# Attention, a first feed-forward layer and a soft mixture of experts on one core: TensorE's order written out up to tile 14, with later slot transposes and sums

## The chip, the cores and the metric

The kernel runs on one core of one Trainium2 chip. The metric is the time of one execution in device microseconds (us), lower is better. Where runs are compared, the median counts.

## What is computed

Three blocks, one after the other, in float32. The reference, cut to what matters:

```python
# attention: batch 4, 8 heads, 512 local rows, 32 global rows, width 64 per head
s_g = scale * q_g @ concat(k_g, k_l).T            # global rows see everything
out_g = softmax(s_g) @ concat(v_g, v_l)
s_ll = where(|i - j| <= 32, scale * q_l @ k_l.T, -1e9)   # local rows see a band
out_l = softmax(concat(scale * q_l @ k_g.T, s_ll)) @ concat(v_g, v_l)
x = rows of concat(out_g, out_l)                  # 2176 x 512
# first layer with a product behind it
h = x @ w_in                                      # 512 -> 2048
g = maximum(0.01 * h, h)
y = g @ w_out                                     # 2048 -> 512
# soft mixture, 8 experts with 4 slots each
logits = y @ phi                                  # 2176 x 32
d = softmax of logits over the rows; slot_input = d.T @ y
slot_out[e] = maximum(slot_input[e] @ w1[e], 0) @ w2[e]   # 512 -> 1024 -> 512
out = softmax of logits over the slots @ slot_out
```

## The kernel before

The 2176 rows are worked on as 17 tiles of 128: tiles 0 to 15 are the local rows of batches 0 to 3 (four tiles each), tile 16 holds all global rows. The kernel never forms y: it multiplies `w_out` by `phi` once (`pmat`), so that the logits of a tile are `g` times `pmat`, and keeps running sums of the softmax over rows.

**Attention** runs per step, one step for two heads of a batch (four steps per batch). A step has `a_T` (transposes of keys and queries: tiles `kTp`, `qTp` in PSUM, `kT`, `qT` in SBUF), `a_S` (scores `sc`, softmax to `se`), `a_E` (transposes `etp` of the softmax, copied to `eT`) and `a_V` (product with the values into `po`, scaled into `xn`). The last steps of a batch also compute the global rows: `g_S` (scores `gl`, `gg`, softmax `gs`), `g_E` (transposes `get`, `geg`) and `g_V` (product `gpo`, scaled to `xg`, transposed as `gxt`). `step(n)` lists these pieces with weights.

**A tile** t of the first layer: `b_X` transposes its rows (`xtp`) and splits them into a high and a low part; `b_H` computes one quarter f of `h` (512 columns) in the bank `hp` with 12 matmuls, in two halves of 6, after which ScalarE writes the quarter of `g`. For the logits `g` must be transposed. For tiles 10 to 14 (`BLK`) and for the first two quarters of tiles 4 to 9 (`HALF`), `blocks` does it: a DVE transpose into `gb`, then 16 block copies per two quarters, which `MOVE` gives to GpSimd (all 16 of the first two quarters; 6 of the next two, with 5 for DVE and 5 for ScalarE). The third and fourth quarters of tiles 4 to 9 go through TensorE instead, `b_L`, into `gtp`, copied to `gT`.

**Behind the tile** come the steps that `l_items(t)` lists: `b_M` and `b_D1` (logits into `lg`, copied to `lp`), `b_D2` (column sums by a matmul on `lp`, then the exp `st` of the slot softmax on ScalarE and a part of it copied by DVE), `b_D3` (transpose of `st` into `lg`, of which DVE takes `d` and both engines take the row softmax), `b_U` (the product of `d` and `g` into the bank `up`, added to `uacc` by DVE).

PSUM has 8 banks. `tp` is a ring of two that all transposes share (`kTp`, `qTp`, `etp`, `gtp`, `xtp`, `get`, `geg`, `gxt`, and also `gg`). `hb` is a ring of two (`hp`, and `up` up to tile 6), `sc` a ring of two, `po` and `sm` (holds `lg`) one each. A bank can be written again when its last reader is done.

**Order.** ScalarE, DVE, GpSimd and the load queue run the order that a scheduler made when the program was built. For TensorE the order is that of the code inside `manual_schedule` (line 1078): there `merge` mixes the attention steps of batches 2 and 3 with `b_items`, the list of pieces of tiles 4 to 14, by their weights, and `upto` cuts the list where the next tile's transposes need attention. What is left of the list for tiles 11 to 14 (`run(*rest)`) was ordered by the scheduler, with `behind` holding some pieces back. Then tiles 15 and 16 and the experts follow.

Of the kernel before, what the change touches and what calls it, by code (L numbers as in the profile page):

```python
# [8 lines left out]
F32 = mybir.dt.float32  # L9
# [11 lines left out]
def kernel(  # L21
# [15 lines left out]
    nc = tc.nc  # L37
# [517 lines left out]
    def g_E(b):  # L555
        es, rs = gst[b]
        ets = []
        for e in range(2):
            pt = tp("get")
            for T in range(NT):  # L560
                nc.tensor.transpose(pt[:, P * T:P * T + P], es[e][:, P * T:P * T + P], ident)
            et = sa.tile([P, S], F32, tag="eT", name="get", bufs=2)
            nc.vector.tensor_copy(et, pt)
            pg = tp("geg")
            nc.tensor.transpose(pg[0:SG, 0:P], es[e][:, S:S + SG], ident)
            eg = sa.tile([SG, P], F32, tag="geg", name="geg", bufs=2)
            nc.vector.tensor_copy(eg, pg[0:SG, 0:P])
            ets.append((et, eg))
        gst[b].append(ets)

    def g_V(b):
# [3 lines left out]
        for e in range(2):  # L575
# [13 lines left out]
            in1=rs.unsqueeze(2).to_broadcast([P, 2, D]), op=ALU.mult,  # L589
        )  # L590
        pt = tp("gxt")
        nc.tensor.transpose(pt[:, 0:P], xg.rearrange("p e d -> p (e d)"), ident)
# [35 lines left out]
    def step(n):  # L628
# [10 lines left out]
        gv = (2.1, lambda: (g_V(b), load_v(n + 2) if b else None))  # L639
        return [e, (0, lambda: None), v, (1.1, lambda: g_E(b))] + ns + nt + [gv]  # L640

# [30 lines left out]
    hps = {}  # L672

    def b_H(t, f, half=None):
        xh, xl = xt[t]
# [21 lines left out]
        gs = gt[t][:, 512 * f:512 * f + 512]  # L697
        nc.scalar.activation(out=gs, in_=hp, func=AF.Prelu, alpha=0.01)  # L698
        if t in BLK or t in HALF and f < 2:
# [48 lines left out]
    def b_D1(t):  # L748
        lg = b_M(t, range(2, NQ) if t in BLK else range(NQ))
        lp = sb.tile([P, 2 * P], F32, tag="lp", name="lp", bufs=1)[:, 0:P]  # L750
        nc.vector.tensor_copy(lp, lg[:, 0:P])
        ms["lg"] = lg, lp
# [52 lines left out]
    def u_add(ds, last):  # L805

        up = bank("po", "up", 1) if last >= 7 else hb("up")
        later = "u" in ms
# [68 lines left out]
    def j_D(ts):  # L877
# [17 lines left out]
        u_add(ds, ts[-1])  # L895

    def l_items(t):
        return ([(0.0, lambda: None), (0.6, lambda: b_M(t, range(2)))] if t in BLK else [
            (0.0, lambda: None) if t in HALF else (0.9, lambda: (b_L(t, 0), b_L(t, 1))),
            (0.9, lambda: (b_L(t, 2), b_L(t, 3))),  # L900
        ]) + [
            (1.3, lambda: b_D1(t)),
            (0.3, lambda: b_D2(t)),
            (0.1, lambda: b_D3(t)),
            (1.0, lambda: b_U(t)),
        ]
# [61 lines left out]
    def b_items(t0, t1):  # L968
        its = []
        for t in range(t0, t1):  # L970
# [6 lines left out]
            if t - 1 in BLK:  # L977
                its += h[0:2] + [li[1]] + h[2:4] + [li[2]] + x + [behind(h[4])]
                its += [li[3]] + [behind(x) for x in h[5:8]] + [li[4], li[5]]
                continue  # L980
            its += [h[0], li[1], h[1], li[0], h[2], h[3], li[2]] + x + [h[4], li[3]]
            its += [h[5], h[6], li[4], h[7], li[5]]
        return its

# [92 lines left out]

    with tc.manual_schedule(engines={mybir.EngineType.PE}):
        for b in range(2, B):
            head = upto(b * NT if b == 2 else 3 * NT - 1)  # L1080
            merge(attn[b - 1], head[:-6])
            run(*head[-6:])
    actx.close()
# [85 lines left out]
    load_e(xe.tile([P, 4, CL], F32, tag="e", name="ew"), NE - 1, 4)  # L1169
    run(*rest)  # L1170
    load_next(ys, ys)

# [233 lines left out]
```

## Time and profile before

| | |
|---|---|
| runs | 497.91 us median of 3 (494.53 to 498.0) |
| profiled execution | 497.15 us, span 495.4 us |
| TensorE (PE) busy | 452.7 us, 91% |
| VectorE (DVE) busy | 277.2 us, 56% |
| ScalarE (ACT) busy | 232.9 us, 47% |
| GpSimd (POOL) busy | 160.3 us, 32% |

The span is the part of the execution that the profile covers; 1.8 us lie around it. Shares of busy time are means over stages that differ: batches 0 and 1 of attention with the conversion of the weights up to about 188 us, attention of batches 2 and 3 mixed with tiles 4 to 10 up to about 345 us, tiles 11 to 16 up to about 430 us, then the experts. In a time line each row has its start, its duration, the engine, the line of the kernel, the output and input tiles, shapes and a count. The distance between the starts of two rows shows what a piece took together with a wait behind it.

### The profile page before, as it was taken

How to read it: one execution, taken by the hardware profiler on the slowest of the kernel's cores; microseconds unless marked ns; L12 is line 12 of the kernel's file. 1: busy time of each engine (PE TensorE's matmuls, PEld its weight loads, DVE VectorE, ACT ScalarE, POOL GpSimd, SP SyncE). 2: the span in 40 equal slices, each digit the busy share in tenths (PEclk: the TensorE clock that was granted, in tenths of full speed). 3: DMA queues.
4: the chain of work that ended last, by engine and by line, in shares of the span. 5: the costliest groups of instructions: out<-in, count | busy, mean ns of one | idle time of the engine just before them, and what ended most of it. 6: DMA issues, size and time to landing. Idle time of an engine off the chain costs nothing.

```text
span 495.4 us, 13462 instructions
## 1 busy us (share of the span) xinstructions
PE 452.7 (91%) x5341; PEld 319.9 (65%) x5341; DVE 277.2 (56%) x880; ACT 232.9 (47%) x678; POOL 160.3 (32%) x281
## 2 busy tenths in 40 slices
PE   7968799998989999999879999999999999999982
PEld 5635668676766656776648776778687777743341
DVE  4575879489547677477544656525655532242222
ACT  4666789487755445453144446124434343321021
POOL 2044787333310203541505161506666630000000
PEclk9985699999999999999989999999999999999998
DMA  9999688499655755344331220259320059989997
GB/s 176 215 197 235 218 254 334 161 304 296 211 144 118 147 115 102 72 103 114 76 75 32 58 54 8 86 213 404 150 85 1 2 173 329 384 336 400 348 301 256
DMA packets 111990, 90.23 MB, mean 182 GB/s; under 512 B 75256, under 2 KB 94392, under 8 KB 111928
## 3 DMA queue, kind: packets, MB, share of 16 engines
q1 hardware_dynamic: 110024, 88.33, 61.4%
q10 hardware_dynamic: 1904, 1.05, 0.8%
q8 instruction: 42, 0.69, 0.6%
q14 instruction: 20, 0.16, 0.1%
HBM read 76.68 MB, written 8.65 MB: 172 GB/s over the span
## 4 chain that ended last, share of the span: by engine, by line
PE 65%; DVE 8%; ACT 4%; DMA 3%; SPq 1%; issue 1%; POOL 1%; DVEq 0%; ACTq 0%; POOLq 0%
PE hp L691 31%; PE gtp L728 4%; PE sc L434 3%; PE up L812 3%; PE po L493 2%; PE lg L742 2%; PE ehp L1270 2%; DMA ew<-in_moe_w_dram 2%; DVE se L446 2%; PE etp L473 2%; ACT se L454 2%; PE sop L1304 1%; SPq L1127 1%; PE wotp L345 1%; PE gpo L579 1%
## 5 line engine op out<-in xcount | busy, mean ns | idle before, releaser
L691 PE MATMUL hp<-wi,xxh 128*128 128x512 f32 x512 | 168.5, 411 | 1.5 <-ACT xxh L665 1.4
L691 PEld LDWEIGHTS hp<-wi,xxh 128*128 128x128 f32 x512 | 93.3, 193 | 28.3 <-issue 6.6
L719 POOL COPY g<-gb 32x256 f32<-32x256 f32 x206 | 82.4, 400 | 83.5 <-DVE gb L710 53.5
L691 PE MATMUL hp<-wi,xxl 128*128 128x512 f32 x256 | 101.9, 399 | 0.0
L698 ACT ACTIVATE g<-hp 128x512 f32<-128x512 f32 x60 | 35.5, 594 | 57.6 <-PE hp L691 54.3
L454 ACT ACTIVATE se<-se,nmx 128x128 f32<-128x128 f32 x128 | 49.6, 390 | 15.6 <-DVE nmx L452 15.5
L691 PEld LDWEIGHTS hp<-wi,xxl 128*128 128x128 f32 x256 | 48.9, 191 | 11.7 <-issue 0.8
L200 POOL COPY vw<-vw 32x1664 f32<-32x1664 f32 x10 | 15.7, 1574 | 81.7 <-DMA vw<-in_v_g_dram 39.5
L710 DVE STREAM_TRANSPOSE gb<-g 128x512 f32<-128x512 f32 x32 | 22.6, 708 | 26.0 <-ACT g L698 25.8
L446 DVE CUSTOM_DVE_ANT_0 se<-sc,mask 128x128 f32<-128x128 f32 x128 | 28.8, 285 | 14.1 <-PE sc L434 14.0
L261 POOL TENSOR_TENSOR wn<-wn,rraw 128x512 int32<-128x512 int32 x16 | 23.0, 1448 | 37.9 <-DVE wn L257 31.3
L434 PE MATMUL sc<-kw,qT 64*32 64x128 f32 x1024 | 27.5, 283 | 1.2 <-DVE kw L406 0.5
L261 POOL TENSOR_TENSOR wo<-wo,rraw 128x512 int32<-128x512 int32 x12 | 16.0, 1330 | 32.0 <-DVE wo L257 7.2
L477 DVE COPY eT<-etp 128x512 f32<-128x512 f32 x28 | 18.6, 687 | 11.4 <-PE etp L473 11.4
L434 PEld LDWEIGHTS sc<-kw,qT 64*32 64x32 f32 x1024 | 19.7, 109 | 8.0 <-issue 4.2
L493 PE MATMUL po<-vw,eT 128*32 128x64 f32 x1024 | 21.9, 229 | 2.8 <-issue 2.0
L730 ACT COPY gT<-gtp 128x512 f32<-128x512 f32 x26 | 14.9, 585 | 20.1 <-PE gtp L728 17.6
L454 ACT ACTIVATION_READ_ACCUMULATOR se<-se,nmx 128x1 f32 x128 | 24.1, 189 | 0.0
L493 PEld LDWEIGHTS po<-vw,eT 128*32 128x32 f32 x1024 | 17.5, 115 | 9.3 <-issue 6.7
L473 PE MATMUL etp<-identr,se 128*128 128x128 f32 x128 | 22.4, 300 | 0.2
L405 DVE COPY kw<-kT 128x672 f32<-128x672 f32 x32 | 19.8, 653 | 3.0 <-ACT kT L394 2.6
L251 ACT ACTIVATE rraw<-rraw 128x512 int32<-128x512 uint32 x28 | 18.7, 676 | 4.4 <-DMA rraw<-in_moe_w_out_dram 3.0
(228 smaller groups left out, 765.5 us busy)
## 6 DMA issues: line engine op xcount, KB each, us to landing
ew<-in_moe_w_dram SPq DMA_DIRECT2D x23, 1024.0 KB, 9.4
rraw<-in_moe_w_in_dram SPq DMA_DIRECT2D x16, 512.0 KB, 6.5
ew<-in_moe_w_dram SPq DMA_DIRECT2D x15, 512.0 KB, 8.8
vw<-in_v_l_dram SPq DMA_DIRECT2D x60, 112.0 KB, 3.3
rraw<-in_moe_w_out_dram SPq DMA_DIRECT2D x12, 512.0 KB, 6.0
wo_f<-wo SPq DMA_DIRECT2D x16, 256.0 KB, 3.9
vn<-in_v_l_dram SPq DMA_DIRECT2D x4, 1024.0 KB, 6.2
wo<-wo_f SPq DMA_DIRECT2D x4, 1024.0 KB, 8.0
```

What stands on the lines that cost most here:

```text
L261: nc.gpsimd.tensor_tensor(out=di, in0=di, in1=m, op=ALU.add)
L405: nc.vector.tensor_copy(kw[:, :, 0:96], src)
L434: last_a[0] = nc.tensor.matmul(bks[e][32 * u:32 * u + 32, P * T:P * T + P], qt[64 * e:64 * e + 64, 32 * U:32 * U + 32], kw[win(U) // (NW / ...
L446: nc.vector.tensor_tensor_reduce(out=s[:, T, :], in0=bk[:, P * T:P * T + P], in1=mask[:, 0 if T == 0 else 2 if T == NT - 1 else 1, :], sca ...
L454: exp_last[0] = nc.scalar.activation(out=s[:, T, :], in_=s[:, T, :], func=AF.Exp, bias=nmx[:, e, T:T + 1], accum_out=sm[:, T, e:e + 1],).ins
L473: last_a[0] = nc.tensor.transpose(pt[:, P * T:P * T + P], es[e][:, T, :], ident).ins
L493: last_a[0] = nc.tensor.matmul(pov[32 * u:32 * u + 32, T, e, :], ets[e][:, 32 * U:32 * U + 32], vw[:, win(U), e, :], start=True, stop=True ...
L691: nc.tensor.matmul(hp, a[:, k, :], w[c][:, k, :], start=(n == 0 and half != 1), stop=(n == len(prods) - 1 and half != 0),)
L698: nc.scalar.activation(out=gs, in_=hp, func=AF.Prelu, alpha=0.01)
L710: nc.vector.transpose(out=gb[:, f % 2], in_=gs)
L719: copy(dst[32 * c:32 * c + 32, :, a], src[32 * a:32 * a + 32, :, c])
L728: nc.tensor.transpose(pt[:, P * c:P * c + P], g[:, o:o + P], ident)
```

## The change

The change has five parts, all in the work on tiles 4 to 14.

1. `b_items` writes another order. The transpose of `st` (`b_D3`) and the product `up` (`b_U`) of tile t, which closed the list of tile t + 1, move into the list of tile t + 2, behind its first and its second half quarter; for tiles 10 to 14 only `b_U` moves. The two halves of the logits (first quarters by `blocks`, second by `gT` or `blocks`) are two pieces also for tiles 4 to 9. `behind` is gone from the list.
2. `manual_schedule` stays open until the list of tiles up to 14 has run, so tiles 11 to 14 are in written order as well.
3. For batches 2 and 3, `step` splits the global pieces: `g_E` makes only the two `get`s, `g_G` both `geg`s later, and `g_X` the transpose `gxt` after another piece.
4. `ahead` gives the scheduler a higher priority for the evictions of `hp`, the copy `lp`, and the steps behind `b_D2` and `b_D3` of tiles 4 to 14.
5. `up` of tiles 4 to 6 takes the bank `po` in place of the ring `hb`.

The diff, cut to its core:

```diff
@@ g_E, g_G, g_V, g_X
-            pg = tp("geg")
-            nc.tensor.transpose(pg[0:SG, 0:P], es[e][:, S:S + SG], ident)
...
+            ets.append([et])
+            if b < 2:
+                g_G(b, e, ets)
...
+        gst["x"] = xg
+        if b < 2:
+            g_X(b)
@@ step
-        return [e, (0, lambda: None), v, (1.1, lambda: g_E(b))] + ns + nt + [gv]
+        if b < 2:
+            return [e, (0, lambda: None), v, (1.1, lambda: g_E(b))] + ns + nt + [gv]
+        gg = (0.3, lambda: [g_G(b, e, gst[b][2]) for e in range(2)])
+        return [e, v, (0.8, lambda: g_E(b))] + ns + [gg] + nt + [gv, (0.1, lambda: g_X(b))]
@@ priorities
+    def ahead(t):
+        return tc.high_priority(offset=400) if NT <= t < NTT - 2 else ExitStack()
...
+    def first(f, t):
+        with ahead(t):
+            f(t)
@@ b_D1, u_add, l_items
-        lg = b_M(t, range(2, NQ) if t in BLK else range(NQ))
+        lg = b_M(t, range(2, NQ) if t in BLK or t in HALF else range(NQ))
...
-        up = bank("po", "up", 1) if last >= 7 else hb("up")
+        up = bank("po", "up", 1) if last >= NT else hb("up")
...
-            (0.0, lambda: None) if t in HALF else (0.9, lambda: (b_L(t, 0), b_L(t, 1))),
+            (0.6, lambda: b_M(t, range(2))) if t in HALF else (0.9, lambda: (b_L(t, 0), b_L(t, 1))),
...
-            (0.3, lambda: b_D2(t)),
-            (0.1, lambda: b_D3(t)),
+            (0.3, lambda: first(b_D2, t)),
+            (0.1, lambda: first(b_D3, t)),
@@ b_items
-                its += h[0:2] + [li[1]] + h[2:4] + [li[2]] + x + [behind(h[4])]
-                its += [li[3]] + [behind(x) for x in h[5:8]] + [li[4], li[5]]
+                its += [h[0]] + d3 + [h[1]] + u + [li[1]] + h[2:4] + [li[2]] + x + [h[4]]
+                its += [li[3]] + h[5:8] + [li[4]]
+                d3, u = [], [li[5]]
                 continue
-            its += [h[0], li[1], h[1], li[0], h[2], h[3], li[2]] + x + [h[4], li[3]]
-            its += [h[5], h[6], li[4], h[7], li[5]]
-        return its
+            its += [h[0]] + d3 + [h[1]] + u + [li[1], h[2], h[3], li[0]] + x + [h[4], li[2]]
+            its += [h[5], li[3], h[6], h[7]]
+            d3, u = [li[4]], [li[5]]
+        return its + d3 + u
@@ the mixed stage
-    with tc.manual_schedule(engines={mybir.EngineType.PE}):
+    mctx = ExitStack()
+    mctx.enter_context(tc.manual_schedule(engines={mybir.EngineType.PE}))
...
     run(*rest)
+    mctx.close()
```

What this does to the order of the instructions, at three places. The first is TensorE at tile 5 and the last attention step of batch 2: from the column sums (`lg<-lp`) over the transposes of keys and queries to `up`. Runs of first-layer matmuls (`hp`) are cut to "...". Before:

```order
L757 MATMUL lg<-lp,s_77 128x128
...
L390 MATMUL kTp<-identr,kn 128x128 x4
L390 MATMUL qTp<-identr,qn 128x128 x4
L802 MATMUL lg<-identr,st 128x128
...
L592 MATMUL gxt<-identr,xg 128x128
L812 MATMUL up<-g,d 32x512 x4
```

After:

```order
L572 MATMUL geg<-identr,gs 32x128 x2
L777 MATMUL lg<-lp,s_77 128x128
L390 MATMUL kTp<-identr,kn 128x128 x4
L390 MATMUL qTp<-identr,qn 128x128 x4
...
L604 MATMUL gxt<-identr,xg 128x128
L822 MATMUL lg<-identr,st 128x128
...
L832 MATMUL up<-g,d 32x512 x4
```

The transpose of `st` has moved from right behind `qTp` to behind `gxt`: between the column sums and it stand now the key and query transposes, one half quarter, the forty matmuls of `gpo`, two more half quarters and `gxt`. In front of the column sums the scores `sc` stood directly; now two half quarters, a piece of `lg` and both `geg`s stand between.

The second place is DVE at the step before it in batch 2, around the addition to `uacc` of tile 4. Before:

```order
L819 SCALAR_TENSOR_TENSOR uacc<-uacc,al,up 128x512
L549 TENSOR_SCALAR gsms<-gsms 128x2
L550 RECIPROCAL grs<-gsms 128x2
L405 COPY kw<-kT 128x7x96 x2
L406 COPY kw<-kgT 128x7x32 x2
L501 TENSOR_TENSOR xn<-po,rs 128x4x128
L730 COPY gT<-gtp 128x512
L477 COPY eT<-etp 128x512 x2
```

After:

```order
L839 SCALAR_TENSOR_TENSOR uacc<-uacc,al,up 128x512
L477 COPY eT<-etp 128x512
L729 STREAM_TRANSPOSE gb<-g 128x512
L477 COPY eT<-etp 128x512
L749 COPY gT<-gtp 128x512
```

The addition to `uacc` stood ahead of the key windows `kw`, an attention output and `gT`; now it stands directly ahead of the copies that empty `etp`, with a transpose into `gb` between them. On TensorE `up`, `etp` and `gtp` follow each other there.

The third place is TensorE at the global scores of batch 3, `gl` and `gg`. Before:

```order
L473 MATMUL etp<-identr,se 128x128 x8
L728 MATMUL gtp<-identr,g 128x128 x8
L519 MATMUL gl<-kT,qgT 32x512 x4
L525 MATMUL gg<-kgT,qgT 32x32 x4
L519 MATMUL gl<-kT,qgT 32x512 x4
L525 MATMUL gg<-kgT,qgT 32x32 x4
L691 MATMUL hp<-wi,xxh 128x512 x2
```

After:

```order
L473 MATMUL etp<-identr,se 128x128 x8
L822 MATMUL lg<-identr,st 128x128
...
L519 MATMUL gl<-kT,qgT 32x512 x4
L525 MATMUL gg<-kgT,qgT 32x32 x4
L519 MATMUL gl<-kT,qgT 32x512 x4
L525 MATMUL gg<-kgT,qgT 32x32 x4
L832 MATMUL up<-g,d 32x512 x4
L747 MATMUL gtp<-identr,g 128x128 x8
```

`gtp` has moved from ahead of the global scores to behind them, with only `up` of tile 7 between; the three half quarters that followed `gg` have moved elsewhere. `gg` and `gtp` share the ring `tp`.

## Rows read from the trace of the kernel before

**Rows 1.** Table by stage: stretch, length, busy us (instructions), PEclk, DMA share, GB/s.

```profile
345.00:400.00 55.00, 55.00 (x376) 40.44 (x374) 32.87 (x88) 22.12 (x60) 34.16 (x85) 1.00 0.19 72
400.00:490.00 90.00, 81.88 (x807) 46.92 (x799) 26.86 (x71) 22.13 (x52) 1.19 (x4) 1.00 0.95 332
```

**Rows 2.** Waits of TensorE from 186 to 380 us: total us, times, longest.

```profile
PE lg L802 <- DVE st L767: 3.8, 2, 3.1
PE get L561 <- DVE get L563: 1.4, 2, 0.7
PE gxt L592 <- DVE xg L587: 0.9, 2, 0.5
PE up L812 <- ACT gs L536: 0.8, 1, 0.8
PE xtp L659 <- ACT kT L394: 0.6, 2, 0.3
```

**Rows 3.** Time line of TensorE, 248 to 256 us: start, us, row, count, wait.

```profile
248.84 0.60 PE L390 MATMUL qTp<-identr,qn 128*128 128x128 f32 x4
252.50 0.48 PE L802 MATMUL lg<-identr,st 128*128 128x128 f32 x1 [3.06 <-DVE st L767]
252.63 1.20 PE L691 MATMUL hp<-wi,xxh 128*128 128x512 f32 x2
...
255.47 0.67 PE L579 MATMUL gpo<-vn,get 128*32 128x64 f32 x32
```

**Rows 4.** Time line of ScalarE at the same place.

```profile
248.51 0.40 ACT L454 ACTIVATE se<-se,nmx 128x128 f32<-128x128 f32 x1 [0.67 <-DVE nmx L452]
...
251.60 0.34 ACT L766 ACTIVATE st<-lg,nm 128x128 f32<-128x128 f32 x1
```

**Rows 5.** Table by stage behind that wait (PEclk is the third figure from the end).

```profile
253.00:254.00 1.00, 1.00 (x3) 0.77 (x3) 0.99 (x3) 0.09 (x1) 0.00 (x0) 0.50 0.00 0
```

**Rows 6.** Time line of TensorE at the global rows of batch 2.

```profile
239.87 0.27 PE L565 MATMUL geg<-identr,gs 128*32 128x128 f32 x1
240.81 0.66 PE L561 MATMUL get<-identr,gs 128*128 128x128 f32 x4 [0.68 <-DVE get L563]
```

**Rows 7.** Time line of TensorE: a pair of transposes, then undisturbed work.

```profile
301.59 1.03 PE L473 MATMUL etp<-identr,se 128*128 128x128 f32 x8
...
304.22 1.23 PE L519 MATMUL gl<-kT,qgT 64*32 64x512 f32 x16
...
326.17 0.73 PE L691 MATMUL hp<-wi,xxh 128*128 128x512 f32 x2
...
326.97 0.62 PE L691 MATMUL hp<-wi,xxh 128*128 128x512 f32 x2
...
327.66 1.04 PE L728 MATMUL gtp<-identr,g 128*128 128x128 f32 x8
328.45 0.71 PE L691 MATMUL hp<-wi,xxh 128*128 128x512 f32 x2
```

**Rows 8.** TensorE behind `gg` of batch 3, then ScalarE emptying its banks.

```profile
305.44 0.73 PE L691 MATMUL hp<-wi,xxh 128*128 128x512 f32 x2
...
307.12 0.28 ACT L542 ACTIVATE gs<-gg,gnmx 128x32 f32<-128x32 f32 x1
...
308.05 0.29 ACT L542 ACTIVATE gs<-gg,gnmx 128x32 f32<-128x32 f32 x1
```

**Rows 9.** Time line of DVE: what it does with banks that TensorE filled.

```profile
228.02 0.74 DVE L819 SCALAR_TENSOR_TENSOR uacc<-uacc,al,up 128x512 f32<-128x512 f32 x1
...
231.21 0.69 DVE L501 TENSOR_TENSOR xn<-po,rs 128x512 f32<-128x512 f32 x1 [0.87 <-PE po L493]
...
302.23 1.29 DVE L477 COPY eT<-etp 128x512 f32<-128x512 f32 x2 [1.24 <-PE etp L473]
```

**Rows 10.** GpSimd's copies of a first half of g, then TensorE's `up`.

```profile
363.36 6.94 POOL L719 COPY g<-gb 32x256 f32<-32x256 f32 x16 [3.36 <-PE lg L742]
...
371.99 1.06 PE L812 MATMUL up<-g,d 128*32 128x512 f32 x8
```

More of the change, by code (lines that the diff above doesn't have):

```diff
@@ L563, in g_E, with g_G @@
             nc.vector.tensor_copy(et, pt)
-            pg = tp("geg")
-            nc.tensor.transpose(pg[0:SG, 0:P], es[e][:, S:S + SG], ident)
-            eg = sa.tile([SG, P], F32, tag="geg", name="geg", bufs=2)
-            nc.vector.tensor_copy(eg, pg[0:SG, 0:P])
-            ets.append((et, eg))
-        gst[b].append(ets)
+            ets.append([et])
+            if b < 2:
+                g_G(b, e, ets)
+        gst[b].append(ets)
+    def g_G(b, e, ets):
+        es = gst[b][0]
+        pg = tp("geg")
+        nc.tensor.transpose(pg[0:SG, 0:P], es[e][:, S:S + SG], ident)
+        eg = sa.tile([SG, P], F32, tag="geg", name="geg", bufs=2)
+        nc.vector.tensor_copy(eg, pg[0:SG, 0:P])
+        ets[e].append(eg)
     def g_V(b):
@@ L590, in g_V, with g_X @@
         )
+        gst["x"] = xg
+        if b < 2:
+            g_X(b)
+    def g_X(b):
+        xg = gst.pop("x")
         pt = tp("gxt")
@@ L697, in b_H @@
         gs = gt[t][:, 512 * f:512 * f + 512]
-        nc.scalar.activation(out=gs, in_=hp, func=AF.Prelu, alpha=0.01)
+        with ahead(t):
+            nc.scalar.activation(out=gs, in_=hp, func=AF.Prelu, alpha=0.01)
         if t in BLK or t in HALF and f < 2:
@@ L748, in b_D1 @@
     def b_D1(t):
-        lg = b_M(t, range(2, NQ) if t in BLK else range(NQ))
+        lg = b_M(t, range(2, NQ) if t in BLK or t in HALF else range(NQ))
         lp = sb.tile([P, 2 * P], F32, tag="lp", name="lp", bufs=1)[:, 0:P]
-        nc.vector.tensor_copy(lp, lg[:, 0:P])
+        with ahead(t):
+            nc.vector.tensor_copy(lp, lg[:, 0:P])
         ms["lg"] = lg, lp
@@ L895, in j_D @@
         u_add(ds, ts[-1])
+    def first(f, t):
+        with ahead(t):
+            f(t)
     def l_items(t):
         return ([(0.0, lambda: None), (0.6, lambda: b_M(t, range(2)))] if t in BLK else [
-            (0.0, lambda: None) if t in HALF else (0.9, lambda: (b_L(t, 0), b_L(t, 1))),
+            (0.6, lambda: b_M(t, range(2))) if t in HALF else (0.9, lambda: (b_L(t, 0), b_L(t, 1))),
             (0.9, lambda: (b_L(t, 2), b_L(t, 3))),
@@ L968, in b_items @@
     def b_items(t0, t1):
-        its = []
+        its, d3, u = [], [], []
         for t in range(t0, t1):
@@ L1076, in upto @@
         return head
-    with tc.manual_schedule(engines={mybir.EngineType.PE}):
[L1079 to L1082, printed above, removed]
+    mctx = ExitStack()
+    mctx.enter_context(tc.manual_schedule(engines={mybir.EngineType.PE}))
+    for b in range(2, B):
+        head = upto(b * NT if b == 2 else 3 * NT - 1)
+        merge(attn[b - 1], head[:-6])
+        run(*head[-6:])
     actx.close()
```

## The prediction

> **What bounds the kernel now.** I looked at the page's busy times first: TensorE is busy 91% of the span and no other engine passes 56%, so the question is where TensorE stands still, and in which stage. The table by stage then splits the run [rows 1]. From 345 to 400 us TensorE is busy for all 55.00 us at the full clock, while the DMA engines are busy 0.19 of the time. From 400 us on, the DMA engines are busy 0.95 of the time, moving expert weights, and this stage begins only when TensorE's last tiles free the buffers of the first layer's weights. So what TensorE saves before 400 us should move the whole last stage earlier. The savings must come from 188 to 345 us, where attention of batches 2 and 3 is mixed with first-layer tiles 4 to 10.
>
> The list of waits of TensorE [rows 2] names the stops there: two on DVE's copy of `st` (3.1 and about 0.7 us), two on the copy of `get`, two before `gxt`, one `up` behind the softmax of the global rows. Busy time hides more of them, because matmuls are pipelined, so from here on I compare starts: the time from one row's start to the next, against the same work where nothing disturbs it.
>
> The largest stop, read closely. Between the start of the four `qTp` transposes and the transpose of `st` 3.66 us pass [rows 3], and four such transposes take about 0.42. The cause stands on ScalarE [rows 4]: the exp of `st` runs at 251.60, behind the eight softmax exps that began at 248.51. And the stop costs twice: behind it the granted clock reads 0.50, its lower level of 1.2 GHz [rows 5], so that the next half quarter of the first layer (six matmuls) takes 2.84 us, from 252.63 to 255.47 [rows 3], where 1.49 is usual, 326.17 to 327.66 [rows 7].
>
> **What the change removes.** All terms are of TensorE's own time line.
> - Transpose of `st` of tile 5: from the second to the last step of a tile's chain into the next tile. Now `kTp`, `qTp`, three half quarters, `gpo` (about 2 us) and `gxt` lie between the column sums and it, some 7 us, and ScalarE's order has its exp behind the same exps, but those begin earlier relative to it, because `sc` now stands ahead of two half quarters, `lg` and `geg`. 3.66 - 0.42 = 3.25 us, and the half clock behind it, 2.84 - 1.49 = 1.35 us.
> - `get` and `geg`: before, `geg` took a bank of the two-bank ring `tp` between the two `get`s, so 0.94 us pass from one `geg` to the next `get` [rows 6], of which the transpose itself needs about 0.11. Three such places (two at batch 2, one at batch 3): 3 x 0.83 = 2.5 us. Now both `get`s run together, and `geg` runs after a half quarter. The wait of `xtp` on the second of them is one of the three; with `lg` of 0.46 between, I keep at most 0.05.
> - `gxt`: two half quarters stand ahead of it now, 0.9 us for the two [rows 2].
> - Waits of `up` and the second wait on `st`: 0.8 + 0.7 = 1.5 us [rows 2]. `up` of tiles 4 to 6 leaves the ring `hb`, so it no longer waits for a bank that ScalarE empties behind the global softmax.
> - The pair of `etp` and `gtp`, sixteen transposes one after the other: 2.63 us from 301.59 to 304.22, against 0.79 for eight, 327.66 to 328.45 [rows 7]: 1.05 lost. The same pair stands at tile 4 in the order of before, and I count 0.9 for it. Both pairs are parted.
> Sum removed: 3.25 + 1.35 + 2.5 + 0.9 + 1.5 + 1.95 = 11.45 us.
>
> **What it adds.**
> - Tile 4: `gtp` right behind `kTp` and `qTp`. Of `xtp` in the same position two waits of 0.3 are listed [rows 2]; with what busy time hides of the second bank I take 0.5 us.
> - Tile 5 (batch 2): `up`, `etp`, `gtp` in a row, and DVE's order is `uacc`, `eT`, a transpose into `gb`, `eT`. Let `etp` start at E. `uacc` (0.74) holds DVE until about E + 0.85, the first copy (0.65, of two in 1.29) until E + 1.5, `gb` (as large a tile, so 0.7) until E + 2.2, the second copy until E + 2.85 [rows 9]. The last four transposes of `gtp` so end near E + 3.3 instead of E + 1.6: 1.7 us. If DVE comes to `uacc` early and `gb` waits elsewhere, it is 0.4; if TensorE drops to half clock behind it, 1.7 + 1.35 = 3.05.
> - Tile 8 (batch 3): `gl`, `gg`, `up`, `gtp`. `gg` lies in the ring that `gtp` wants. Before, `gg` ended at 305.44 and its two banks were read out by 307.4 and 308.4 [rows 8], 2.0 and 3.0 us later; that was free, because three half quarters and more followed. Now only `up` (1.0) follows, and ScalarE's new order puts one eviction of `g` (0.5 to 0.6) between the two, so 3.5 for the second bank. `gtp` ends at about 3.9 instead of 1.8 us behind `gg`: 2.1 us. Bounds: 0.9 if only the first bank counts, 3.45 with the half clock.
> - Smaller: `kTp` behind `geg` (0.25), `qTp` behind `etp` at tile 6 (0.2), `up` of tile 4 behind `d` (0.15): 0.6 us, bounds 0 and 2.
> - TensorE changes four times more often between a first-layer run and something else, and a restart costs about 0.1: of a half quarter the first three matmuls take 0.80 us and the next three 0.69 [rows 7]. With the halved `lg` I take 0.5 us.
> Sum added: 0.5 + 1.7 + 2.1 + 0.6 + 0.5 = 5.4 us.
>
> **What costs nothing, and its cover.** From tile 10 on, the first half of `lg` runs 2.9 us earlier. It needs the sixteen GpSimd copies of that half: 363.36 + 6.94 = 370.3, and it would stand behind `up`, which starts at 371.99 and takes 1.0 [rows 10]. That leaves 2.7 us of cover. `up` after the second half quarter also delays the first eviction of the next tile (the buffer `g` has two turns) by 1 us, covered by the three half quarters until that bank returns. Loads are triggered by the same transposes as before, and nothing in [rows 2] waits for one.
>
> Sum against the profiled run's own time: 497.15 - 11.45 + 5.4 = 491.1 us; that run lies 0.8 below the median of 497.91, within their spread, so I leave it at 491.1.
>
> **A bank shared.** `up` of tiles 4 to 6 now shares the one bank `po` with the attention outputs. DVE's product into `xn` empties `po` and takes 0.69 us [rows 9]; with some 0.15 until it starts, an `up` right behind `po` would stop for about 0.85, three of them for 2.5. In the new order at least a half quarter (1.49) and the transpose of `st` stand between, so I charge only the 0.15 above. The Trainium skill, "Perfetto Trace Analysis", section "Matmuls" under tensor performance, says that independent matmul groups should rotate through different PSUM banks, so that one is emptied while the next group runs; by that rule leaving the ring of two banks is a step back, and the sum would be 493.6 instead of 491.1. No row here shows an `up` behind `po` on one bank in these tiles.
>
> **Rivals.**
> 1. *The waits only change place.* With two banks for all transposes, each eviction that DVE or ScalarE reaches late is a stop. If both new stops reach the length at which the clock falls (3.05 + 3.45), the small ones cost 2, and one more stop of 1.5 shows up, 5.4 becomes 11.0: 496.7 us. For it: DVE's and ScalarE's orders were changed by priority, and `sm`, which needs all eight exps, now stands ahead of `eT` at tile 6. Against: the slack that I count at the other places is 0.5 us or more at all but two.
> 2. *`up` stops for `po`*, three times 0.85: 493.6 us. For it: DVE often stands in other work when `po` ends. Against: the half quarter between.
> 3. *The new stops hardly show* (0.4, 0.9, and 0 of the small ones): 5.4 becomes 2.3, 488.0 us.
> 4. *The gain does not arrive at the end.* If the DMA stage after 400 us ran by the landing of its loads alone, the end would stay at 497. Against: those loads cannot start before TensorE frees their buffers.
> 5. *Slower: DVE's order starves the ring.* Eight attention steps each pass two evictions through DVE behind softmax sums. If that stop is like the one of [rows 3] with its clock (3.25 + 1.35 = 4.6), then two such places already cost more than the gain, 500.3, and from three on the kernel is slower by over 1%: 491.1 + 3 x 4.6 = 504.9 us. The slack that I count at those places is 0 to 3 us, so a single one is possible, three are not likely.
>
> **How the numbers follow.** Forecast 0.53 (488.5 to 493.5 alone), rival 1 0.17, rival 2 0.05, rival 3 0.12, rival 4 0.06, rival 5 0.07. The predicted time is 491.1. The range 487.0 to 496.8 leaves out rival 5, most of 4 and the low end of 3. Within 1% of 497.9 (492.9 to 502.9) is about what a measurement of this kernel cannot tell from no change. Faster: most of the forecast (0.46) and rival 3, 0.58; same: the rest of the forecast, rivals 1, 2 and 4, 0.35; slower: rival 5, 0.07.
>
> **What would show it.** In the profile after: no stop over 1 us before a transpose of `st`, and a granted clock of 1.00 in all of batch 2's attention; starts of `get` and `get` 0.45 apart; a stop of about 1 us and another inside `gtp` behind `gg` at batch 3, and a slow `etp`/`gtp` pair at batch 2; TensorE reaching tile 11 some 6 us earlier, and the same length from there to the end. Wrong would be: the clock at 0.50 in a new place, TensorE waiting on GpSimd copies before `lg` in tiles 10 to 14, or a last stage longer than before.

## The result, and the profile after

The changed kernel takes 490.13 us (median of 4 runs, 489.67 to 491.9) against 497.64 us (4 runs), a ratio of 0.987 with the 95% interval 0.982 to 0.992. A second series of the same code gave 492.4 us (6 runs, 489.57 to 493.89) against 497.76 us and the same ratio, 0.987 (0.982 to 0.992). The gain of 1.3% is thus clear of no change; that it is over 1% is likely and not certain. The profiled execution takes 490.33 us with a span of 488.6 us; TensorE is busy 451.3 us of it, 92%. The forecast of 491.1 us stands 1.0 us off the first series and 1.3 us off the second.

Where the 6.8 us of span went is read between two rows that both kernels have: the last `up` ahead of the mixed stage (its operand is `gx`), and `up` of tile 13. The time line of TensorE after:

```profile
185.95 1.06 PE L832 MATMUL up<-gx,d 128*32 128x512 f32 x8
...
392.75 1.06 PE L832 MATMUL up<-g,d 128*32 128x512 f32 x8
```

That is 206.80 us. Before:

```profile
186.91 1.06 PE L812 MATMUL up<-gx,d 128*32 128x512 f32 x8
...
399.51 1.06 PE L812 MATMUL up<-g,d 128*32 128x512 f32 x8
```

That is 212.60 us. So the changed stretch is 5.8 us shorter, and another 1.0 us lies ahead of it, where the order is the same; over the fourteen traces of this case the first of the two rows starts anywhere from 185.5 to 187.4, so that 1.0 is spread and no effect. From the second row to the end of the span it is 95.85 us after and 95.89 before.

The list of TensorE's waits from 186 to 400 us (total us, times, longest), to be laid beside [rows 2]:

```profile
PE gtp L747 <- ACT gs L542: 1.9, 2, 1.2
PE gtp L747 <- DVE eT L477: 1.0, 2, 0.5
PE xtp L674 <- ACT kT L394: 0.5, 2, 0.3
PE xtp L674 <- DVE eT L477: 0.4, 1, 0.4
...
```

The waits on `st`, `get` and `xg` are gone. New are two pairs, both at `gtp`: behind `gg`, on the exp `gs`, and behind `etp`, on `eT`. (Before, too, `gtp` waited for `eT`, 0.7 us in two, but at other pairs, those of tiles 4 and 8, which the change parts.) The table by stage (stretch, length, busy us of TensorE, its weight loads, DVE, ScalarE and GpSimd, then granted clock, DMA share and GB/s) has them in its second and third row:

```profile
186.00:230.00 44.00, 43.40 (x582) 32.97 (x579) 27.33 (x110) 21.93 (x79) 17.63 (x35) 1.00 0.41 82
230.00:260.00 30.00, 28.98 (x435) 21.19 (x433) 17.13 (x54) 10.49 (x34) 9.46 (x18) 1.00 0.46 108
260.00:300.00 40.00, 37.84 (x534) 27.97 (x519) 26.39 (x112) 21.82 (x83) 16.05 (x34) 1.00 0.19 37
...
345.00:400.00 55.00, 54.75 (x374) 40.59 (x373) 31.30 (x82) 23.59 (x59) 32.95 (x82) 1.00 0.15 51
```

The granted clock is 1.00 in all of them; the half clock of [rows 5] does not occur. Where the 3.06 us stop of [rows 3] stood, the transpose of `st` passes without a wait, 0.02 us from its start to the next:

```profile
252.22 0.27 PE L604 MATMUL gxt<-identr,xg 128*128 128x128 f32 x1
252.33 0.27 PE L822 MATMUL lg<-identr,st 128*128 128x128 f32 x1
252.35 0.71 PE L709 MATMUL hp<-wi,xxh 128*128 128x512 f32 x2
```

The first new stop, at tile 5, in the time line of TensorE:

```profile
229.53 1.06 PE L832 MATMUL up<-g,d 128*32 128x512 f32 x8
230.52 1.09 PE L473 MATMUL etp<-identr,se 128*128 128x128 f32 x8
232.06 0.66 PE L747 MATMUL gtp<-identr,g 128*128 128x128 f32 x4 [0.45 <-DVE eT L477]
233.26 0.66 PE L747 MATMUL gtp<-identr,g 128*128 128x128 f32 x4 [0.54 <-DVE eT L477]
233.67 0.70 PE L709 MATMUL hp<-wi,xxh 128*128 128x512 f32 x2
```

And in that of DVE, which empties the two banks of the ring `tp`:

```profile
230.66 0.75 DVE L839 SCALAR_TENSOR_TENSOR uacc<-uacc,al,up 128x512 f32<-128x512 f32 x1
231.32 0.68 DVE L477 COPY eT<-etp 128x512 f32<-128x512 f32 x1
231.92 0.70 DVE L729 STREAM_TRANSPOSE gb<-g 128x512 f32<-128x512 f32 x1
232.55 0.65 DVE L477 COPY eT<-etp 128x512 f32<-128x512 f32 x1
```

DVE's four rows run without a gap, and the last `gtp` starts when the fourth is through: sixteen transposes take 3.15 us, from 230.52 to 233.67. The second, at the global scores of batch 3, on TensorE:

```profile
296.01 0.29 PE L525 MATMUL gg<-kgT,qgT 64*32 64x32 f32 x16
296.24 1.06 PE L832 MATMUL up<-g,d 128*32 128x512 f32 x8
298.45 0.66 PE L747 MATMUL gtp<-identr,g 128*128 128x128 f32 x4 [1.15 <-ACT gs L542]
299.88 0.66 PE L747 MATMUL gtp<-identr,g 128*128 128x128 f32 x4 [0.77 <-ACT gs L542]
```

And on ScalarE, whose two exps `gs` empty the banks of `gg`:

```profile
298.03 0.28 ACT L542 ACTIVATE gs<-gg,gnmx 128x32 f32<-128x32 f32 x1
...
298.29 0.59 ACT L717 ACTIVATE g<-hp 128x512 f32<-128x512 f32 x1
...
299.43 0.30 ACT L542 ACTIVATE gs<-gg,gnmx 128x32 f32<-128x32 f32 x1
```

`gtp` is through at 300.29, 4.05 us after `up` began right behind `gg`, where `up` and eight transposes alone would take 1.8.

### The profile page after: what moved, and what is told of

Its sections match the earlier page's. It is cut to its first block, busy times and chain, and to the rows that moved or that the text cites. A ratio compares the mean times of both kernels' runs of the same rounds, so it can differ in the third digit from the quotient of the medians.

```text
span 488.6 us, 13462 instructions
## 1 busy us (share of the span) xinstructions
PE 451.3 (92%) x5341; PEld 316.7 (65%) x5341; DVE 275.7 (56%) x880; ACT 234.2 (48%) x678; POOL 160.0 (33%) x281
## 3 DMA queue, kind: packets, MB, share of 16 engines
q10 hardware_dynamic: 1904, 1.05, 0.8%
## 4 chain that ended last, share of the span: by engine, by line
PE 74%; ACT 7%; DMA 6%; DVE 5%; SPq 4%; issue 2%; POOL 1%; DVEq 0%; ACTq 0%; POOLq 0%
PE hp L709 37%; DMA rraw<-in_moe_w_in_dram 4%; PE gtp L747 3%; PE sc L434 3%; PE ehp L1298 3%; PE up L832 3%; PE po L493 2%; PE lg L761 2%; PE etp L473 2%; PE xtp L674 1%; PE wotp L345 1%; PE sop L1332 1%; SPq L162 1%; PE gpo L585 1%; ACT se L454 1%
## 5 line engine op out<-in xcount | busy, mean ns | idle before, releaser
L709 PEld LDWEIGHTS hp<-wi,xxh 128*128 128x128 f32 x512 | 92.1, 191 | 24.2 <-issue 5.3
L747 PE MATMUL gtp<-identr,g 128*128 128x128 f32 x112 | 16.9, 281 | 4.7 <-ACT gs L542 1.9
```

The lines of the kernel that those rows point to most:

```text
L709: nc.tensor.matmul(hp, a[:, k, :], w[c][:, k, :], start=(n == 0 and half != 1), stop=(n == len(prods) - 1 and half != 0),)
L747: nc.tensor.transpose(pt[:, P * c:P * c + P], g[:, o:o + P], ident)
```

## The experiments

The theory: the gain is the sum of stops removed, less the two new stops at `gtp`. Against it stood that the gain comes from one part alone, that the shared bank `po` eats some of it, and that the parts thought to be free are not. In the table "stretch" is the distance between the two rows named above. Each group of four lines is set against the kernel before on its own chip: medians 497.04 us for the first four lines, 497.93 for the next four, 497.76 for the last four.

| kernel | us | ratio to before (95%) | stretch, us |
|---|---|---|---|
| glob_whole: changed kernel, global steps whole | 496.1 | 0.999 (0.995 to 1.002) | 211.90 |
| before_split: kernel before, global steps split | 490.15 | 0.983 (0.979 to 0.987) | 207.30 |
| slots_early: changed kernel, `st` and `up` not later | 501.78 | 1.008 (1.004 to 1.011) | 217.08 |
| gt_sel: changed kernel, two `gtp` one half quarter later | 488.3 | 0.979 (0.974 to 0.984) | 204.50 |
| no_prio: changed kernel, no priorities | 493.4 | 0.991 (0.989 to 0.994) | 209.58 |
| up_hb: changed kernel, `up` in ring `hb` | 492.2 | 0.988 (0.983 to 0.993) | 208.36 |
| slots_early_hb: slots_early, `up` in ring `hb` | 501.56 | 1.006 (1.003 to 1.009) | 217.08 |
| gt_sel_hb: gt_sel, `up` in ring `hb` | 488.28 | 0.980 (0.977 to 0.984) | 204.22 |
| after_again: the changed kernel | 492.4 | 0.987 (0.982 to 0.992) | 207.18 |
| sched_tail: changed kernel, tiles 11 to 14 scheduled | 522.96 | 1.049 (1.043 to 1.056) | - |
| lg_whole: changed kernel, `lg` of tiles 4 to 9 in one piece | 497.62 | 1.001 (0.998 to 1.004) | 212.26 |
| gt_sel2: gt_sel, `gtp` of tile 8 two half quarters later | 486.38 | 0.977 (0.972 to 0.983) | 203.34 |

(A dash: the scheduler gives `up` of tile 13 another place there, with 97.9 us to the end of the span instead of 95.1 to 96.2, so the distance would compare different work.)

### The split of the global steps, taken out and done alone

Taken out of the changed kernel (glob_whole), and put alone into the kernel before (before_split, which gets the new `g_E`, `g_G`, `g_X` and `step` and nothing else). The edit of glob_whole:

```diff
-            if b < 2:
-                g_G(b, e, ets)
+            g_G(b, e, ets)
...
-        if b < 2:
-            g_X(b)
+        g_X(b)
...
-        if b < 2:
+        if True:
             return [e, (0, lambda: None), v, (1.1, lambda: g_E(b))] + ns + nt + [gv]
```

> The changed kernel with the global steps of batches 2 and 3 whole again, as before the change (get, geg, get, geg in a row, gxt right behind gpo). Theory (each geg between the two get costs 0.83 us of a bank, each gxt 0.45): 3 to 4 stops of 0.8 and two of 0.45 come back, 3.3 us or more: 493.4 us; the transpose of st of tile 5 still has no stop and the clock stays at 1.00. Rival (the gain is all in the later slots): 490.1 us.

> The kernel before with one part of the change alone: the global steps of batches 2 and 3 split. Theory (stops add up by place): the three stops of 0.83 us around get and geg go, the stops of gxt too (0.9 us in all), and because the column sums of tile 5 now come behind kTp and qTp and gpo stands between them and the transpose of st, most of the 3.25 us stop with its half clock (1.35 us) goes as well: 497.6 - 2.5 - 0.9 - 3.5 = 490.7, up to 493 if the stop only moves. Rival (without the later slots the stop of st stays whole, with the half clock): 494.3 us.

glob_whole gives back 5.1 us of stretch (211.90 against 206.80), more than its theory expected (3.3 us or more, 493.4 us against the 496.1 measured), and its list of waits names the places:

```profile
...
PE get L561 <- DVE get L563: 1.4, 2, 0.7
...
PE gxt L602 <- ACT qT L394: 0.9, 1, 0.9
PE etp L473 <- DVE eT L477: 0.8, 1, 0.8
...
PE gxt L602 <- DVE xg L592: 0.4, 1, 0.4
```

No wait on `st` is listed, so the rest of the change removes that stop without the split. But before_split removes most of it too, without any later slot: what was 3.06 us [rows 3] is 0.74 there, and the clock stays at 1.00.

```profile
PE lg L817 <- DVE st L782: 1.5, 2, 0.8
PE gtp L743 <- DVE eT L477: 0.7, 2, 0.3
...
```

The time line of ScalarE there shows why (first of the eight softmax exps, then the exp of `st`):

```profile
242.47 0.40 ACT L454 ACTIVATE se<-se,nmx 128x128 f32<-128x128 f32 x1 [0.77 <-DVE nmx L452]
...
245.57 0.35 ACT L781 ACTIVATE st<-lg,nm 128x128 f32<-128x128 f32 x1
```

The scores `sc` now stand ahead of `xtp` and no longer behind two `geg`s, so the softmax exps begin 0.18 us behind the start of the column sums (242.29). Before, they began 3.19 us behind it (245.32 to 248.51, [rows 4]), and the exp of `st` waited for them. Split alone: a ratio of 0.983. All parts: 0.987. All parts but the split: 0.999. So the split carries the gain, and the other four parts together add nothing that these runs can tell from zero. That zero is a balance: they remove the stop on `st` as well, and bring in the two stops at `gtp`. With these taken away (gt_sel2 below), the stretch is 4.0 us shorter than with the split alone (203.34 against 207.30).

### The later places of `st` and `up`, and the bank of `up`

slots_early keeps everything but the later places. up_hb is the changed kernel with `up` of tiles 4 to 6 back in its old ring, and slots_early_hb has both edits:

```diff
...
-            its += [h[0]] + d3 + [h[1]] + u + [li[1], h[2], h[3], li[0]] + x + [h[4], li[2]]
-            its += [h[5], li[3], h[6], h[7]]
-            d3, u = [li[4]], [li[5]]
+            its += [h[0], h[1], li[1], h[2], h[3], li[0]] + x + [h[4], li[2]]
+            its += [h[5], li[3], h[6], li[4], h[7], li[5]]
...
-        up = bank("po", "up", 1) if last >= NT else hb("up")
+        up = bank("po", "up", 1) if last >= 7 else hb("up")
```

> The changed kernel with the transpose of st and up back at the end of the next tile's list; split global steps, priorities and written tail stay. Theory (the later place takes the exp of st off TensorE's line): a stop of about 2.2 us before the transpose of st right behind the global scores of batch 2, and one near 1 us at tile 6; at tile 8 up no longer stands in front of gtp but a half quarter does, so 1 to 1.5 us of that stop go, and the stop of up, etp, gtp at tile 5 shrinks to 1; 491.5 to 492.5 us, and half clock only if a stop reaches 3 us. Rival A (the later slots carry most of the gain): 494.5 us or more. Rival B (the priority has the exp early enough anyway): 490 us or less.

> The kernel with the last transposes of a tile's chain and its up inside the next tile as before (501.8 us), now also with up of tiles 4 to 6 in the ring hb. Theory (the shared bank po is one part of its loss, the two stops of 1.40 and 0.81 us at po and up; the stops on st, 3.9 us, and the 0.7 us per tile at tiles 11 to 13 stay): 499.6 us. Rival (the bank also drives the stops on st, because DVE waits in it): 496 us or less. Rival 2 (the bank is beside the point): 501.8 us.

> The changed kernel with the product up of tiles 4 to 6 back in the ring hb of the first layer's banks, so that it no longer shares the bank po with the attention outputs; orders of TensorE, ScalarE and DVE the same. Theory (in the changed kernel up stands at least one half quarter behind po, so the shared bank costs nothing): 490 us, within 1 us of the changed kernel. Rival (the shared bank costs up to 0.85 us at each of three tiles, hidden in busy time): 487.5 to 489 us. Third: ring hb is then short of a bank and hp stops: 491 to 492 us.

slots_early is slower than the kernel before, and 9 us slower than its theory had it; only rival A (494.5 us or more) leaves room for it. Its waits:

```profile
PE lg L822 <- DVE st L787: 3.9, 3, 2.0
PE po L493 <- DVE uacc L839: 1.4, 1, 1.4
...
PE up L832 <- DVE xn L501: 0.8, 1, 0.8
...
```

The new order puts the column sums one half quarter later; with `b_D3` left in its old place only one half quarter of matmuls lies between the column sums and the transpose, and the stops on `st` come back. In tiles 11 to 13 `up` now follows the transpose of `st` directly and waits 0.28 us for `d`, and each of these tiles takes 14.85 us from `up` to `up` instead of 14.14. The later places are thus what the rest of the new order needs, not a gain on top of it. The second and third line are the shared bank: where `up` and `po` follow each other directly, one waits for DVE to empty the bank of the other. In slots_early_hb both are gone, and from `up` to the next row at that place it is 0.88 us instead of 2.46. Yet the kernel is no faster (501.56 us, the number of the rival by which the bank is beside the point), and the stretch is 217.08 us in both traces. Two things took the gain back in the trace. One is a new stop on `st` at tile 6, ahead of the place where `up` no longer waits for `po`:

```profile
273.21 0.33 PE L822 MATMUL lg<-identr,st 128*128 128x128 f32 x1 [0.61 <-DVE st L787]
```

The other is the clock: behind the same 2.00 us stop on `st` just ahead of this place it stayed at 1.00 in slots_early and fell to 0.50, the level of 1.2 GHz, in slots_early_hb (table by stage):

```profile
227.00:228.00 1.00, 1.00 (x3) 0.79 (x3) 0.53 (x3) 0.37 (x2) 0.00 (x0) 0.50 0.00 0
```

so that the next six matmuls took 2.71 us instead of 1.46. The expectation of slots_early tied the half clock to a stop of 3 us; 2.00 us was enough here. How far the clock explains the medians, and not only these two traces, is not shown.

In the changed kernel itself the bank costs nothing. From `up` of one tile to that of the next, for tiles 4 to 7, up_hb takes 24.38, 20.60 and 21.70 us and the changed kernel 24.39, 20.61 and 21.71. Its trace is 1.6 us longer for another reason, again the clock: orders, and the stops of 1.15 and 0.77 us at `gtp` of tile 8, are the same, and behind them the table reads, first up_hb (whose stop ends at 302.01), then the changed kernel (300.29), in which no such stretch from 150 to 400 us is below 1.00:

```profile
302.00:303.00 1.00, 1.00 (x4) 0.82 (x3) 0.00 (x0) 0.59 (x1) 0.00 (x0) 0.50 0.06 16
```

```profile
302.00:303.00 1.00, 1.00 (x65) 0.91 (x59) 0.00 (x0) 0.00 (x0) 0.00 (x0) 1.00 0.00 0
```

The six matmuls behind the stop took 2.75 us in up_hb and 1.56 in the changed kernel. The median of 492.2 us is near the number that the third expectation gave to a ring short of a bank, but the list of waits has none of `hp`.

### Priorities, the piece of `lg`, the written order of tiles 11 to 14

Three parts that the forecast took to be worth nothing, each undone alone. First the priorities, then the piece of `lg` (its weight in the list goes too), then the written order:

```diff
-        return tc.high_priority(offset=400) if NT <= t < NTT - 2 else ExitStack()
+        return tc.high_priority(offset=400) if False else ExitStack()
```

> The changed kernel without its priorities (the Prelu of the first layer, the copy lp and the two routing steps are no longer put ahead for tiles 4 to 13); TensorE's order stays the same row for row, and only some ten rows of ScalarE and thirty of DVE stand elsewhere. Theory (the priorities hardly matter, since TensorE stopped nowhere on lp, d or the Prelu in the changed kernel): 490 us, within 1 us of the changed kernel, list of waits the same to within 0.5 us. Rival (they are what keeps the Prelu and lp ahead of the softmax work): stops of hp on the Prelu or of lg on lp appear, 493 us or more.

```diff
-        lg = b_M(t, range(2, NQ) if t in BLK or t in HALF else range(NQ))
+        lg = b_M(t, range(2, NQ) if t in BLK else range(NQ))
...
-            (0.6, lambda: b_M(t, range(2))) if t in HALF else (0.9, lambda: (b_L(t, 0), b_L(t, 1))),
+            (0.0, lambda: None) if t in HALF else (0.9, lambda: (b_L(t, 0), b_L(t, 1))),
```

> The changed kernel with the routing product lg of tiles 4 to 9 in one piece again, behind the second slot transposes, instead of a first half ahead of them. Theory (the split of lg fills no gap of its own; it only moves 0.55 us of matmuls): 490 us, within 1 us of the changed kernel. Rival (the first half of lg is what stands between etp, get, or gg and the next transposes, and hides DVE's copies there): xtp waits for eT at two or three places by 0.5 us more, 491 to 492 us.

```diff
+    mctx.close()
     actx.close()
...
     run(*rest)
-    mctx.close()
```

> The changed kernel with the written order of TensorE ended after the mixed stage, so that tiles 11 to 14 of the first layer are ordered by the scheduler again, as before the change; the stage up to 330 us is the same. Theory (that part of the change is worth nothing, since TensorE was busy without a break there before too): 490 us, within 1 us of the changed kernel. Rival (the written order saves stops there): 492 us or more, with waits of up or lg in the list from 345 to 400 us.

All three theories (that the part is worth nothing) were wrong. **Without the priorities** TensorE's order is the same, but at tile 7 the exp of `st` stands behind the eight softmax exps again, and DVE copies `eT` ahead of `st`. The list of waits shows a stop that the changed kernel does not have, and two others grow:

```profile
...
PE lg L822 <- DVE st L787: 1.3, 1, 1.3
PE xtp L674 <- ACT kT L394: 1.2, 2, 0.9
...
PE lg L761 <- ACT ce L814: 0.7, 1, 0.7
...
```

The rival has the number (493 us or more) but not the cause: its stops of `hp` and on `lp` did not come. The stretch is 2.8 us longer than in the first trace of the changed kernel and 2.4 longer than in its second; the intervals of the ratios (0.989 to 0.994, and 0.982 to 0.992) overlap, so the size rests on the traces.

**With `lg` in one piece** all of the gain is lost, more than the rival's 491 to 492 us. TensorE stops for 3.26 us at `etp` of the second step of batch 3:

```profile
282.47 1.14 PE L473 MATMUL etp<-identr,se 128*128 128x128 f32 x8 [3.26 <-ACT gT L749]
```

ScalarE shows what is late (the last of the eight exps, then the two copies that empty the ring):

```profile
281.47 0.39 ACT L454 ACTIVATE se<-se,nmx 128x128 f32<-128x128 f32 x1
...
281.85 1.04 ACT L749 COPY gT<-gtp 128x512 f32<-128x512 f32 x2
```

In the changed kernel these two copies ran at 276.28, ahead of the exps. The piece itself need not be the cause: without its weight the merge put `etp` one half quarter closer to `gtp`, and the scheduler then put the exps first on ScalarE; no run keeps the weight without the piece. So this run shows the price of that order (3.3 us, six matmuls at 2.61 us behind it, and 1.1 us at another `etp`), and not that a split `lg` is worth it anywhere else.

**With tiles 11 to 14 left to the scheduler** the kernel is 5% slower; the rival (492 us or more, waits of `lg` and `up`) has the kind of loss but not its size. TensorE runs all 24 matmuls of a half tile together and the chain of small steps behind the logits together too, with nothing in between:

```profile
360.11 0.48 PE L822 MATMUL lg<-identr,st 128*128 128x128 f32 x1 [2.75 <-DVE st L787]
360.87 1.93 PE L832 MATMUL up<-g,d 128*32 128x512 f32 x8 [0.28 <-DVE d L809]
363.52 1.22 PE L709 MATMUL hp<-wi,xxh 128*128 128x512 f32 x2 [0.72 <-ACT g L717]
```

The clock reads 0.50 from 360 to 369 us. From one `up` to the next it is 22.28 us (360.87 to 383.15) where the written order takes 14.14. The kernel before also left these tiles to the scheduler, with `behind` and without the priorities, and took 13.76 us for two of them; which of these two protected it was not tried. Written order does not beat that: from `up` of tile 10 to that of tile 13 it takes 42.42 us (350.33 to 392.75) against 41.71 before (357.80 to 399.51). The 0.7 us more are no loss, for three transposes `xtp` of 0.41 us lie in it where before only one did; the others ran earlier. For the same work the two are about equal.

### The two new stops, taken away

gt_sel moves `gtp` behind one half quarter at tiles 5 and 8, gt_sel2 behind two and `po` at tile 8 (shown), gt_sel_hb is gt_sel with `up` in the ring `hb`:

```diff
-            its += [h[0]] + d3 + [h[1]] + u + [li[1], h[2], h[3], li[0]] + x + [h[4], li[2]]
+            l = [h[2], li[1], h[3]] if t == 6 else [h[2], h[3], li[1]] if t == 9 else [li[1], h[2], h[3]]
+            its += [h[0]] + d3 + [h[1]] + u + l + [li[0]] + x + [h[4], li[2]]
```

> The changed kernel with one edit: at tiles 5 and 8 the transposes gtp stand one half quarter later, so that a half quarter (1.5 us) lies between up and gtp. Theory (the two new stops of the change are the ring of two transpose banks, emptied late by DVE behind uacc and by ScalarE behind the global softmax): the stop at tile 5 goes (1.5 us), that at tile 8 falls from 2.25 to about 0.6 us; 490.1 becomes 487.0 us, and nothing else moves. Rival (the engines that empty the banks are themselves late, so the stop comes at the next transposes or at po instead): 489.5 to 490.5 us.

> The changed kernel with gtp one half quarter later at tiles 5 and 8 (488.3 us), now also with up of tiles 4 to 6 in the ring hb. Theory (nothing left at that bank): 488.3 us, within 0.8 us. Rival (shared bank costs time that busy time hides): 486.5 us or less.

> The changed kernel with gtp of tile 5 one half quarter later, and gtp of tile 8 two half quarters later, behind po. Theory (the last 0.56 us of the stop behind gg goes, nothing else moves): 487.7 us, 0.6 below the version with both one half quarter later (488.3). Rival (gT then comes too late from ScalarE, so that the second half of lg waits): 488.5 us or more, a wait of lg on gT in the list.

gt_sel takes 488.3 us, between what the theory and its rival gave. Its stretch is 2.3 us shorter than that of the changed kernel; the stop at `eT` is gone, the one behind `gg` is left with 0.56:

```profile
PE gtp L747 <- ACT gs L542: 0.6, 1, 0.6
```

In gt_sel2 it is gone as well, and `gtp` of tile 8 runs whole:

```profile
299.62 1.09 PE L747 MATMUL gtp<-identr,g 128*128 128x128 f32 x8
```

Its stretch is another 1.2 us shorter and its median 486.38 us (forecast 487.7), a ratio of 0.977 (0.972 to 0.983), the lowest of all kernels here, though the intervals of gt_sel and before_split overlap it. With 3.5 us of stretch the two stops cost about what their rows say, 1.57 and 2.25. No wait of `lg` on `gT` appeared. gt_sel_hb is equal to gt_sel.

### The changed kernel a second time

> The changed kernel itself a second time, unchanged, with a second profile. Question: in two traces of other kernels with the same order of TensorE around the stop of gtp behind gg (1.15 and 0.77 us), the clock stayed at 1.00 in one and read 0.50 behind it in the other. Theory (whether the clock falls behind such a stop differs from execution to execution, and is worth 1.2 to 1.6 us): single times of this kernel spread over some 1.5 to 3 us, and this trace shows the clock at 0.50 behind the stop in some or no place, with the same list of waits; ratio to before 0.985 to 0.99. Rival (the clock is set by the order alone): the same clock of 1.00 in every stretch from 150 to 400 us, times within 1 us of 490.1.

The second trace has the same list of waits and the clock at 1.00 from 150 to 400 us; its stretch is 0.4 us longer. Single times spread by 4.3 us (489.57 to 493.89). That the slower ones are executions in which the clock fell behind a stop, as in the trace of up_hb, would fit, but only the profiled executions show their clock row by row, and this one shows no fall. One more trace bears on it: sched_tail has the same order of TensorE and the same two stops up to and at tile 8, and there the clock fell behind them (table by stage):

```profile
302.00:303.00 1.00, 1.00 (x3) 0.35 (x2) 0.00 (x0) 0.00 (x0) 0.00 (x0) 0.50 0.00 0
```

So the fall is possible with the order of the changed kernel; whether it makes its slower executions stays open.

## Why the prediction was right, and where it was not

**The end follows the stretch.** From `up` of tile 13 to the end of the span it is between 95.1 and 96.2 us in the thirteen traces where it has the same place, while that row moves from 388.84 to 404.45. Rival 4 (the gain does not arrive) is out.

**What was removed**, as starts against starts in the two traces. The transpose of `st` at tile 5 with the half clock behind it: 3.31 + 1.27 = 4.6 us, forecast 4.6. `get`, `geg` and `xtp` of batch 2 took 2.88 us (239.37 to 242.25) and take 1.19, those of batch 3 took 2.00 and take 1.18: 2.5 us, forecast 2.5. `gxt`: 1.3 us, forecast 0.9, because busy time hid part of both stops. The waits of `up` and the second `st`: 0.88 + 0.94 = 1.8 us, forecast 1.5. The pairs of `etp` and `gtp`: 0.87 + 1.05 = 1.9 us, forecast 1.95. A wait of `up` of tile 7 on `d`, 0.4 us, was overlooked. Sum 12.6 us, forecast 11.45.

**What was added.** Tile 4: 0.7 us, forecast 0.5. Tile 5: 1.57, forecast 1.7; DVE went through the four steps in the order that the forecast wrote down and within 0.2 us of its times (last `gtp` through at E + 3.15, forecast E + 3.3). Tile 8: 2.25, forecast 2.1, with the two banks read out 2.1 and 3.5 us behind `gg` (forecast 2.0 and 3.5). The small ones: 0.5, forecast 0.6. That makes 5.0 us, and 12.6 - 5.0 = 7.6, where the stretch lost only 5.8. The 1.8 us between, a remainder, stand against the term of the forecast for restarts and the halved `lg`, 0.5: this term was sized too small by 1.3 us. Most of it can be read: ten whole `lg` took 10.09 us before, from start to start, and their twenty halves take 11.34, 1.25 us more. The gains that the forecast missed, 1.1 us, hid the error, so that the sum came out this close is in part luck.

**The cause of the large term was told too narrowly.** The forecast counted the 4.6 us at `st` under the later place of its transpose, and named the earlier start of the softmax exps only as a help. The later place is enough without the split (glob_whole), but so, nearly, is the split without the later place, which the forecast priced at 2.5 + 0.9 us only: with `sc` earlier on TensorE, the softmax exps begin 3 us earlier against the column sums, and alone it brings a ratio of 0.983 and 5.3 us of stretch (before_split). One stop was removed by two parts of the change, and the sum, which counted it once, came out right for the whole and would have been wrong for each part: without the split it gives 11.45 - 3.4 - 5.4 = 2.65 us, and glob_whole's stretch is 0.7 us shorter than before.

**The rivals.** Rival 1 (both new stops with the clock down, and more behind) did not come in either trace of the changed kernel; up_hb and sched_tail show that the clock can fall there. Rival 2 (`up` stops for `po`) did not happen, for the reason given, the half quarter between; slots_early shows the price where that is missing: 0.81 us for `up` behind `po`, near the 0.85 that was taken, and 1.40 for `po` behind `up`, a case that was not priced. The Trainium skill, "Perfetto Trace Analysis", section "Matmuls", says that independent matmul groups should rotate through different PSUM banks. These two waits in slots_early agree with it; in the changed kernel sharing a bank cost nothing (0.01 us per tile against up_hb), since other work stands between. Rival 3 (the new stops hardly show, 0.4 and 0.9 us) is wrong: they cost 1.57 and 2.25. Rival 5 (a stop on ScalarE or DVE like that of [rows 3]) did not come in the changed kernel, but it is one edit away: no_prio and lg_whole each have one. (The four stops of 2.8 us on `st` in sched_tail have another cause, a chain of small steps with nothing between.)

**What was taken as free.** The cover that the forecast named for the GpSimd copies held, since no wait on them is listed. But the priorities and the written tail were never priced at all, and taking one away costs 2.4 to 2.8 us and 30 us. A part that adds nothing over the kernel before can still be what the other parts stand on.

## What to carry to other kernels

Where one engine runs a written order and the others a scheduled one, look for each wait at what stands ahead of the releasing instruction on its own engine: here the large stops of the kernel before, of no_prio and of lg_whole came from a softmax's eight exps (3.1 us) standing ahead of one short exp or copy. Price a change of order as a whole and by start-to-start distances against undisturbed work, since two edits can remove the same stop; to learn what a part is worth, do it alone and also undo it alone. Two blocks of transposes in a row through a ring of two banks want other matmuls between them: here one half quarter took away the stop behind `etp`, two the stop behind `gg`, together 3.5 us.

## What was not expected of the hardware

The granted clock does not follow from the order and the stops alone. Behind stops of the same length at the same place it fell to 0.50 in one trace and stayed at 1.00 in another, at two places: after 2.00 us it fell in slots_early_hb and not in slots_early, and after 1.15 and 0.77 us at tile 8 it fell in two (up_hb and sched_tail) of the seven traces that have these stops. Each of the three falls cost about 1.6 us on TensorE's time line (at tile 8 in up_hb, 25.84 us from `up` to `up` instead of 24.29), as much as the edit under test, so single traces of two kernels should be compared stretch by stretch with the clock beside each, before a difference of that size is put down to an edit.
